# Output weights of seven kv heads read in 8 KB rows, results brought to that layout

## The chip, the cores and the metric

The kernel runs on one core of a Trainium2 chip. The metric is device time in microseconds (us) of one execution. Lower is better.

## The reference, cut to what matters

The program sums three terms for one decode step of a batch of 8: the input, grouped-query attention over a cache of 8192 positions, and a token mixer. Everything is float32.

```python
# B=8, D=512, Hq=32, Hkv=8, Sk=8192, Dh=128, F=1792; S=1 token
xn = layernorm(x)
q = (xn @ wq)                       # 32 heads of 128; 4 query heads share a kv head
scores = q . k * Dh**-0.5           # k_cache: (8, 8, 8192, 128), 268 MB
o = softmax(scores) @ v             # v_cache: the same size
attn = concat(o) @ wo               # wo: (4096, 512), 8.4 MB
h = layernorm(xn)
u = gelu(h * w1 + b1)               # for each of 512 channels, 1792 wide
y = sum(u * w2) + b2
out = x + attn + y
```

The two caches and the two weight matrices make 554 MB, each byte of which is read once.

## The kernel before

**Items and steps.** The work is cut into 64 items, one for each pair of kv head h and batch row b (item i = 8h + b). An item has one 4 MB tile of k and one of v. Partition p of such a tile holds 64 consecutive positions, that is 32 KB that lie in one piece in memory. An item is worked in four chunks of 16 positions a partition, and one chunk is one step of the main loop at the end of the kernel (256 steps and a few to run out). A step s calls `t_half` twice (TensorE transposes the k chunk s + 1, ScalarE and VectorE copy one half each out of PSUM), then `qk` (scores of chunk s), then `pv` (values of the chunk nine steps back, LAG = 9). Everything else is hung on a step and a place in it by `at(step, place, function)`: the softmax of an item (`sm_max`, `sm_bias`, `sm_exp`, `sm_place`, `sm_sum`), `o_place` two steps after the item's last `pv`, the projections `q_project`, `q_place` and `o_project` once for each kv head, and the mixer for batch row b = h (`mx_begin`, 14 times `mx_step`, `mx_end`). Each engine runs its instructions in this written order.

**Transfers.** All large loads are issued by SyncE, in one queue. The tiles `raw` of k and v come from a pool of five buffers (RING = 5), so that `load_next` (line 65) has up to five tiles under way or in use, and issues the next when `t_half` has done with a k tile or `pv` with a v tile. The queue also carries the query weights (`load_wq`, line 80) and the output weights (`load_wo`, line 86) of each kv head, 1 MB each, into one shared buffer `wqo`. A query weight row is a 2 KB piece. The output weights of one kv head are 512 rows of 512 numbers, and `load_wo` puts row r\*128 + p on partition p at place r: four separate pieces of 2 KB on each partition, one for each of the four query heads.

**From the values to the output.** `pv` leaves an item's result in PSUM in blocks (partition: position group, step and head; columns: four blocks of 128), ScalarE scales it by the softmax sum into `ob`, and `o_place` (line 294) sums the blocks that belong together. For each of the four blocks TensorE takes the 128x128 block as weights and four columns of the constant `ohu` as the moving operand, so that a 128x4 result has the 128 components of a head on the partitions and the four query heads in the columns. VectorE copies it to column `BS * b` of `OT[h]`. After the eight items of a kv head, `o_project` (line 305) multiplies `OT[h][:, r, :]` with `wos[h][:, r, :]` over r = 0 to 3 and adds the sum to `yacc`.

**Shared places.** PSUM has one buffer `misc` for all the small products, SBUF one buffer `sq` (the query rows of `q_project` and the scratch of `sm_bias`) and one buffer `g` (of `mx_step`). `mx_begin` spreads a normalized row over all partitions by one matmul with 8 partitions of `ident` as weights and the 512 columns of `hn` moving.

Of the kernel before, what the change touches and what calls it, by code (L numbers as in the profile page):

```python
# [8 lines left out]
F32 = mybir.dt.float32  # L9
AF = mybir.ActivationFunctionType  # L10
ALU = mybir.AluOpType
AX = mybir.AxisListType
PSUM = bass.MemoryType.PSUM

B, D, HQ, HKV, SK, DH, F = 8, 512, 32, 8, 8192, 128, 1792
REP = HQ // HKV
P = 128
# [3 lines left out]
CG = 4  # L21
GT = CH_T // CG
GW = P // CG
BS = GW // B
NC = D // P
# [13 lines left out]
def attn_mixer_kernel(ctx: ExitStack, tc: tile.TileContext, x, kc, vc, wq, wo, w1, b1, w2, b2, out):  # L39
    nc = tc.nc  # L40
    const = ctx.enter_context(tc.tile_pool(name="const", bufs=1))
    ring = ctx.enter_context(tc.tile_pool(name="ring", bufs=RING))
    ktp = ctx.enter_context(tc.tile_pool(name="ktp", bufs=2))
    work = ctx.enter_context(tc.tile_pool(name="work", bufs=2))
    one = ctx.enter_context(tc.tile_pool(name="one", bufs=1))
# [6 lines left out]
    def misc():  # L52
        return ps_m.tile([P, 512], F32, name="misc")
# [31 lines left out]

    def load_wo(h):
        t = one.tile([P, REP, D], F32, name="wqo")
        nc.sync.dma_start(t, wo[h * REP * DH:(h + 1) * REP * DH, :].rearrange("(r p) n -> p r n", p=P))
        wos[h] = t

    load_next()
# [14 lines left out]
    quarter = [slice(j * D // CG, (j + 1) * D // CG) for j in range(CG)]  # L106


    ident = const.tile([P, P], F32, name="ident")
# [8 lines left out]
    nc.vector.tensor_scalar(hmask, ohw, 1.0, 3.0e38, op0=ALU.subtract, op1=ALU.mult)  # L118
    ohu = const.tile([P, GT * REP], F32, name="ohu")
    nc.vector.tensor_reduce(ohu, ident.rearrange("p (j x) -> p x j", x=GW)[:, :GT * REP, :], AX.X, ALU.add)  # L120
    oh2 = work.tile([P, REP], F32, name="oh2")
    nc.vector.tensor_reduce(oh2, ident.rearrange("p (g x) -> p x g", x=2 * REP)[:, :REP, :], AX.X, ALU.add)
    lmask = const.tile([P, 1], F32, name="lmask")
# [2 lines left out]
    nc.vector.tensor_scalar(ohl, ohw, lmask, None, op0=ALU.mult)  # L126
    epst = const.tile([B, 1], F32, name="epst")
    nc.vector.memset(epst, EPS)
    bsel = const.tile([P, B, GW], F32, name="bsel")
    nc.vector.memset(bsel, 0.0)  # L130
    for b in range(B):
        nc.vector.memset(bsel[:, b, BS * b:BS * b + 1], 1.0)
    spread = const.tile([B, GW], F32, name="spread")
    nc.vector.memset(spread, 0.0)
    nc.vector.tensor_copy(spread.rearrange("b (c s) -> b c s", s=BS)[:, :, 0], ident[:B, :B])
# [6 lines left out]
    for k in range(2):  # L142
        t = const.tile([P, PW + GW - GT * REP], F32, name=f"pt{k}")
# [3 lines left out]
    for k in range(2):  # L147
        t = const.tile([P, REP, GW], F32, name=f"ot{k}")
# [4 lines left out]
    def layer_norm(dst, src):  # L153
        st = work.tile([B, 6], F32, name="st")
        nc.vector.bn_stats(st, src)
        mv = work.tile([B, 2], F32, name="mv")
        nc.vector.bn_aggr(mv, st)
        sd = work.tile([B, 1], F32, name="sd")
        nc.scalar.activation(sd, mv[:, 1:2], AF.Sqrt, bias=epst)
        rs = work.tile([B, 1], F32, name="rs")  # L160
        nc.vector.reciprocal(rs, sd)
        nc.vector.tensor_scalar(dst, src, mv[:, 0:1], rs, op0=ALU.subtract, op1=ALU.mult)

    xn = t2k.tile([B, D], F32, name="t2k")
    layer_norm(xn, x_sb)
    hn = const.tile([B, D], F32, name="hn")
    layer_norm(hn, xn)
    yx = t2k.tile([B, D], F32, name="t2k")
    nc.vector.tensor_scalar(yx, x_sb, b2t, None, op0=ALU.add)
# [122 lines left out]
    OT = {}  # L292

    def o_place(i):
        h, b = divmod(i, B)
        if b == 0:
            OT[h] = OTS[h % 2]
        m = misc()
        ob = OB.pop(i)
        for u in range(GT):  # L300
            nc.tensor.matmul(m[:, :REP], ob[:, u * DH:(u + 1) * DH], ohu[:, u * REP:(u + 1) * REP],  # L301
                             start=(u == 0), stop=(u == GT - 1))
        nc.vector.tensor_copy(OT[h][:, :, BS * b], m[:, :REP])
# [10 lines left out]
    mx = {}  # L314

    def mx_begin(b):
        m = misc()
        nc.tensor.matmul(m, ident[:B, b:b + 1].to_broadcast([B, P]), hn, start=True, stop=True)  # L318
        hb = one.tile([P, D], F32, name="hb")
        nc.scalar.copy(hb, m)  # L320
        acc = one.tile([P, D], F32, name="macc")
        nc.gpsimd.memset(acc, 0.0)
        mx[b] = (hb, acc)
# [8 lines left out]
    def mx_end(b):  # L332
        m = misc()
        for j in range(CG):
            nc.tensor.matmul(m[j * GW:(j + 1) * GW, :D // CG], bsel[:, b, :], mx[b][1][:, quarter[j]],
                             start=True, stop=True)
        nc.vector.tensor_add(yacc, m[:, :D // CG], yacc)

# [6 lines left out]
    for i in range(N_IT):  # L345
        s = (i + 1) * NCH
        at(s - 1, 2, sm_max, i)
        at(s, 3, sm_bias, i)
        at(s + 1, 1, sm_exp, i)
        at(s + 1, 3, sm_place, i)  # L350
        at(s + 2, 3, sm_sum, i)
        at(s + LAG + (2 if i < N_IT - 2 else 0), 3, o_place, i)
    HS = B * NCH
    for h in range(HKV):
        s = h * HS
        if h + 1 < HKV:
            at(s + LAG + 4, 3, load_wq, h + 1)
            at(s + LAG + 9, 2, q_project, h + 1)
            at(s + LAG + 10, 2, q_place, h + 1)
        at(s + LAG + 12, 3, load_wo, h)  # L360
        at(s + HS + LAG + 3, 2, o_project, h)
        at(s + 3, 2, mx_begin, h)
        for k in range(NF):
            at(s + 4 + k + k // 2, 1 + 2 * (k % 2), mx_step, h, k)
        at(s + 28, 2, mx_end, h)
# [5 lines left out]
    m = misc()  # L371
    for c in range(NC):
        nc.tensor.transpose(m[:, c * B:(c + 1) * B], xn[:, c * P:(c + 1) * P], ident[:B, :B])
    nc.vector.tensor_copy(xnT[:, :, :B], m[:, :NC * B].rearrange("p (c b) -> p c b", b=B))
    for j in range(CG):
        nc.tensor.matmul(m[j * GW:(j + 1) * GW, GT * GW:GT * GW + D // CG], spread, yx[:, quarter[j]], start=True, stop=True)
    nc.vector.tensor_copy(yacc, m[:, GT * GW:GT * GW + D // CG])
# [41 lines left out]
```

## Time and profile before

| | |
|---|---|
| median of three runs | 1308.89 us (1308.6 to 1309.88) |
| profiled execution | 1308.48 us |
| its span, first to last instruction | 1306.7 us |
| mean granted TensorE clock | 0.957 |
| DMA | 555.13 MB in 28164 packets, mean 425 GB/s |

The profile is one execution. "Busy" of an engine is the time in which it has an instruction at work. PE is TensorE, PEld its weight loads, DVE is VectorE, ACT is ScalarE, POOL is GpSimd and SP is SyncE. A DMA is cut into packets, one for each piece that is contiguous on both sides, and the packets of a DMA are shared out over 16 DMA engines. The share of a DMA queue is the time that its packets took, divided by 16 times the length of the stretch.

### The profile page before, as it was taken

Reading aid. Unit: us, or ns where it says so; the run is one execution under the profiler, and the core shown is the slowest. Engines: PE = TensorE matmul, PEld = TensorE weight load, DVE = VectorE, ACT = ScalarE, POOL = GpSimd, SP = SyncE. Lnnn points to the kernel's source line nnn. Section 1 sums busy time; section 2 is a strip of 40 time slices with the busy share of each in tenths; the row PEclk is TensorE's granted clock in tenths of the full one; section 3 lists DMA queues with packets and bytes.
Section 4 is the critical chain, followed back from the end, with each engine's and each line's share of the span. In section 5 each row is a group of like instructions: output and inputs, shape, how many; then the busy total and the mean of one; then the engine's idle time right before and its main releaser. Section 6 shows DMA issues by size and latency. Waiting matters only on the chain.

```text
span 1306.7 us, 22347 instructions
## 1 busy us (share of the span) xinstructions
PE 1162.4 (89%) x9852; PEld 715.8 (55%) x9852; DVE 407.4 (31%) x646; ACT 587.8 (45%) x740; POOL 227.0 (17%) x242
## 2 busy tenths in 40 slices
PE   6979899798998989979898898998989979899988
PEld 4545555455554655546555555554645546555554
DVE  4423233232332333323333233322323323233321
ACT  2654244552545525445254452554525535255532
POOL 1322002220122201222012220122201221012310
PEclk8999999998999999999999898999989989899999
DMA  9999999999999999999999999999999999999995
GB/s 402 432 431 431 428 430 432 429 429 433 432 431 428 429 431 432 432 433 427 433 432 430 430 429 433 433 431 429 429 431 430 433 429 432 432 432 432 432 427 223
DMA packets 28164, 555.13 MB, mean 425 GB/s; under 512 B 2556, under 2 KB 2588, under 8 KB 11172
## 3 DMA queue, kind: packets, MB, share of 16 engines
q1 hardware_dynamic: 27924, 553.67, 98.8%
q8 instruction: 77, 1.26, 0.4%
q14 instruction: 19, 0.16, 0.0%
q0 software_dynamic: 128, 0.02, 0.0%
q10 hardware_dynamic: 16, 0.02, 0.0%
HBM read 553.69 MB, written 0.02 MB: 424 GB/s over the span
## 4 chain that ended last, share of the span: by engine, by line
DMA 56%; PE 39%; ACT 3%; DVE 1%; issue 1%; POOL 0%; SPq 0%; ACTq 0%; DVEq 0%; POOLq 0%
DMA raw<-in_A_k_cache_dram 37%; DMA wqo<-in_A_wq_dram 17%; PE pt L202 16%; PE acc L220 8%; PE acc L276 8%; PE misc L301 3%; DMA raw<-in_A_v_cache_dram 3%; PE misc L177 1%; ACT L242 1%; PE misc L249 1%; ACT kt L203 1%; ACT t2k L242 1%; PE misc L318 1%; PE misc L257 1%; PE misc L309 1%
## 5 line engine op out<-in xcount | busy, mean ns | idle before, releaser
L202 PE MATMUL pt<-ident,raw 128*128 128x128 f32 x4096 | 515.9, 281 | 67.6 <-DMA raw<-in_A_k_cache_dram 67.1
L202 PEld LDWEIGHTS pt<-ident,raw 128*128 128x128 f32 x4096 | 478.0, 147 | 74.5 <-issue 56.0
L203 DVE COPY kt<-pt 128x1024 f32<-128x1024 f32 x256 | 313.5, 1225 | 618.3 <-PE pt L202 505.4
L203 ACT COPY kt<-pt 128x1024 f32<-128x1024 f32 x256 | 258.8, 1011 | 455.7 <-PE pt L202 322.9
L220 PE MATMUL acc<-kt,z 128*32 128x512 f32 x2048 | 279.0, 617 | 0.0
L276 PE MATMUL acc<-raw,pt 128*32 128x512 f32 x2040 | 273.0, 608 | 2.5 <-DMA raw<-in_A_v_cache_dram 2.5
L329 POOL TENSOR_SCALAR g<-g,w2t 128x512 f32<-128x512 f32 x112 | 77.5, 692 | 876.6 <-ACT g L328 876.6
L276 PEld LDWEIGHTS acc<-raw,pt 128*32 128x32 f32 x2040 | 65.3, 113 | 143.6 <-issue 118.1
L330 POOL TENSOR_TENSOR macc<-macc,g 128x512 f32<-128x512 f32 x112 | 142.3, 1271 | 9.3
L328 ACT ACTIVATE g<-hb,b1t,w1t 128x512 f32<-128x512 f32 x112 | 91.1, 813 | 11.5 <-POOL macc L330 10.9
L289 ACT ACTIVATE t2k<-acc,rl 128x512 f32<-128x512 f32 (+1 forms) x65 | 44.0, 679 | 108.5 <-PE acc L276 104.6
L301 PEld LDWEIGHTS misc<-ohu,t2k 128*128 128x128 f32 x512 | 61.9, 191 | 55.0 <-DVE kt L203 31.0
L249 PEld LDWEIGHTS misc<-ident,t2k 128*128 128x128 f32 x256 | 26.8, 140 | 82.5 <-ACT t2k L242 76.7
L301 PE MATMUL misc<-ohu,t2k 128*128 128x4 f32 x512 | 67.3, 255 | 0.7 <-ACT t2k L289 0.6
L220 PEld LDWEIGHTS acc<-kt,z 128*32 128x32 f32 x2048 | 40.7, 109 | 44.5 <-issue 44.4
L249 PE MATMUL misc<-ident,t2k 128*128 128x128 f32 x256 | 42.0, 286 | 25.5 <-ACT t2k L242 25.5
L242 ACT ACT_TABLE_LOAD x48 | 61.6, 1283 | 0.8
L328 ACT ACT_TABLE_LOAD x48 | 61.6, 1283 | 0.8
L257 PEld LDWEIGHTS misc<-lr,ohl 128*128 128x128 f32 x128 | 20.1, 197 | 59.1 <-issue 50.7
L177 PE MATMUL misc<-wqo,xnT 128*32 128x128 f32 x256 | 15.5, 420 | 38.8 <-DMA wqo<-in_A_wq_dram 38.3
L250 ACT COPY pt<-misc 128x256 f32<-128x256 f32 x64 | 23.7, 370 | 58.1 <-PE misc L249 58.1
L233 PEld LDWEIGHTS misc<-ident,mr 128*128 128x128 f32 x128 | 19.0, 187 | 53.7 <-DVE kt L203 38.6
(67 smaller groups left out, 285.6 us busy)
## 6 DMA issues: line engine op xcount, KB each, us to landing
raw<-in_A_k_cache_dram SPq DMA_DIRECT2D x63, 4096.0 KB, 30.0
raw<-in_A_v_cache_dram SPq DMA_DIRECT2D x63, 4096.0 KB, 33.2
wqo<-in_A_wq_dram SPq DMA_DIRECT2D x8, 1024.0 KB, 30.6
wqo<-in_A_wo_dram SPq DMA_DIRECT2D x8, 1024.0 KB, 28.3
raw<-in_A_k_cache_dram SPq DMA_DIRECT2D x4, 1024.0 KB, 10.2
raw<-in_A_v_cache_dram SPq DMA_DIRECT2D x1, 2048.0 KB, 29.1
raw<-in_A_v_cache_dram SPq DMA_DIRECT2D x1, 1024.0 KB, 31.2
raw<-in_A_v_cache_dram SPq DMA_DIRECT2D x1, 512.0 KB, 31.9
```

The source lines that it names most:

```text
L202: nc.tensor.transpose(pt[:, t * P:(t + 1) * P], KR[n // NCH][:, n % NCH * CH_T + k * w + t, :], ident)
L203: (nc.vector.tensor_copy if k else nc.scalar.copy)(KT[n][:, k * w * P:(k + 1) * w * P], pt)
L220: nc.tensor.matmul(S[i][j * GW:(j + 1) * GW, :], w, kt[:, j * 512:(j + 1) * 512], start=(c == 0), stop=(c == NCH - 1))
L242: nc.scalar.activation(p, S.pop(i), AF.Exp, bias=st[i], scale=SCALE, accum_out=lr)
L249: nc.tensor.transpose(m[:, u * P:(u + 1) * P], p[:, u * P:(u + 1) * P], ident)
L257: nc.tensor.matmul(m[:, :1], ohl, st.pop(i)[1], start=True, stop=True)
L276: nc.tensor.matmul(O[i][j * GW:(j + 1) * GW, :], w, v[:, j * 512:(j + 1) * 512], start=(c == 0), stop=(c == NCH - 1))
L289: nc.scalar.activation(ob[:, x], o[:, x], AF.Copy, scale=rl)
L301: nc.tensor.matmul(m[:, :REP], ob[:, u * DH:(u + 1) * DH], ohu[:, u * REP:(u + 1) * REP], start=(u == 0), stop=(u == GT - 1))
L328: nc.scalar.activation(g, hb, AF.Gelu_apprx_tanh, bias=b1t[:, j:j + 1], scale=w1t[:, j:j + 1])
L329: nc.gpsimd.tensor_scalar(g, g, w2t[:, j:j + 1], 1.0, op0=ALU.mult, op1=ALU.mult)
L330: nc.gpsimd.tensor_add(acc, acc, g)
```

## The change

`load_wo` reads the weights of the first seven kv heads so that partition p holds the rows 4p to 4p + 3, which lie together in memory: one piece of 8 KB a partition. The last kv head keeps the old layout. `OT[h]` must follow: partition p now stands for head p // 32 and components 4 (p mod 32) to 4 (p mod 32) + 3. For these heads `o_place` takes a new constant matrix `pick` (128x128 for each block) as the weights and the block itself, 128 columns, as the moving operand. This gives a 128x128 result in which row p holds all 128 components of head p // 32. A mask `keep` lets four of them stand, and a sum over strided columns brings them to 128x4.

Room in SBUF for `pick` and `keep` comes from two edits. The constant `bsel` becomes one strip that is read at a shifting offset in place of eight copies, and `hn` becomes a passing tile in the buffer of `g`. For that the rows of `hn` are transposed at the start to `hnT` (four small transposes and a copy), and `mx_begin` spreads a row with four matmuls with a 128x128 weight each and 128 columns of `ident` moving.

```diff
@@ load_wo
         t = one.tile([P, REP, D], F32, name="wqo")
-        nc.sync.dma_start(t, wo[h * REP * DH:(h + 1) * REP * DH, :].rearrange("(r p) n -> p r n", p=P))
+        how = "(r p) n -> p r n" if h == HKV - 1 else "(p r) n -> p r n"
+        nc.sync.dma_start(t, wo[h * REP * DH:(h + 1) * REP * DH, :].rearrange(how, p=P))
         wos[h] = t
@@ constants
+    pick = const.tile([P, GT, P], F32, name="pick")
+    nc.vector.tensor_copy(pick.rearrange("p u (h g) -> p (u h) g", h=REP),
+                          ohu.unsqueeze(2).to_broadcast([P, GT * REP, GW]))
+    own = work.tile([P, GW], F32, name="own")
+    nc.vector.tensor_reduce(own, ident.rearrange("p (j x) -> p x j", x=GW), AX.X, ALU.add)
+    keep = const.tile([P, P], F32, name="keep")
+    nc.vector.tensor_copy(keep.rearrange("p (g c) -> p g c", c=REP), own.unsqueeze(2).to_broadcast([P, GW, REP]))
@@
-    bsel = const.tile([P, B, GW], F32, name="bsel")
+    BO = BS * (B - 1)
+    bsel = const.tile([P, BO + GW], F32, name="bsel")
     nc.vector.memset(bsel, 0.0)
-    for b in range(B):
-        nc.vector.memset(bsel[:, b, BS * b:BS * b + 1], 1.0)
+    nc.vector.memset(bsel[:, BO:BO + 1], 1.0)
@@
-    hn = const.tile([B, D], F32, name="hn")
+    hn = one.tile([B, D], F32, name="g")
@@ o_place
         m = misc()
         ob = OB.pop(i)
+        if h < HKV - 1:
+            for u in range(GT):
+                nc.tensor.matmul(m[:, :DH], pick[:, u, :], ob[:, u * DH:(u + 1) * DH],
+                                 start=(u == 0), stop=(u == GT - 1))
+            t = one.tile([P, P], F32, name="sq")
+            nc.vector.tensor_tensor(t, m[:, :DH], keep, op=ALU.mult)
+            nc.vector.tensor_reduce(OT[h][:, :, BS * b], t.rearrange("p (g c) -> p c g", c=REP), AX.X, ALU.add)
+            return
         for u in range(GT):
@@ mx_begin
-        nc.tensor.matmul(m, ident[:B, b:b + 1].to_broadcast([B, P]), hn, start=True, stop=True)
+        for c in range(NC):
+            nc.tensor.matmul(m[:, c * P:(c + 1) * P], hnT[:, c, b:b + 1].to_broadcast([P, P]), ident, start=True, stop=True)
@@ mx_end
-            nc.tensor.matmul(m[j * GW:(j + 1) * GW, :D // CG], bsel[:, b, :], mx[b][1][:, quarter[j]],
+            nc.tensor.matmul(m[j * GW:(j + 1) * GW, :D // CG], bsel[:, BO - BS * b:BO - BS * b + GW], mx[b][1][:, quarter[j]],
@@ before the main loop
+    hnT = const.tile([P, NC, B], F32, name="hnT")
+    for c in range(NC):
+        nc.tensor.transpose(m[:, P + c * B:P + (c + 1) * B], hn[:, c * P:(c + 1) * P], ident[:B, :B])
+    nc.vector.tensor_copy(hnT, m[:, P:P + NC * B].rearrange("p (c b) -> p c b", b=B))
```

## Rows read from the trace of the kernel before

**Rows 1.** The page: engines' busy time; GB/s in 40 slices; packets; queues.
```profile
PE 1162.4 (89%) x9852; PEld 715.8 (55%) x9852; DVE 407.4 (31%) x646; ACT 587.8 (45%) x740; POOL 227.0 (17%) x242
...
GB/s 402 432 431 431 428 430 432 429 429 433 432 431 428 429 431 432 432 433 427 433 432 430 430 429 433 433 431 429 429 431 430 433 429 432 432 432 432 432 427 223
DMA packets 28164, 555.13 MB, mean 425 GB/s; under 512 B 2556, under 2 KB 2588, under 8 KB 11172
...
q1 hardware_dynamic: 27924, 553.67, 98.8%
q8 instruction: 77, 1.26, 0.4%
```
**Rows 2.** TensorE in the list of waits: who waited for whom, total us, times, longest.
```profile
PE pt L202 <- DMA raw<-in_A_k_cache_dram: 67.1, 31, 5.6
...
PE misc L177 <- DMA wqo<-in_A_wq_dram: 38.3, 7, 6.2
```
**Rows 3.** DMAs issued from 110 to 111 us: KB each, us to landing.
```profile
raw<-in_A_k_cache_dram SPq DMA_DIRECT2D x1, 4096.0 KB, 25.9
wqo<-in_A_wo_dram SPq DMA_DIRECT2D x1, 1024.0 KB, 28.1
```
**Rows 4.** SyncE's issues: start, us, what.
```profile
26.26 0.33 SPq L72 DMA_DIRECT2D raw<-in_A_v_cache_dram  x1
...
110.11 0.33 SPq L72 DMA_DIRECT2D raw<-in_A_k_cache_dram  x1
110.49 0.73 SPq L88 DMA_DIRECT2D wqo<-in_A_wo_dram  x1
```
**Rows 5.** The chain that ended last, its end: start, us, what.
```profile
1242.59 36.84 DMA raw<-in_A_v_cache_dram
...
1279.57 1.06 PE acc L276 x8
...
1303.24 0.29 DVE yacc L311
```
**Rows 6.** The DMA view, 135.6 to 136.2 us (0.6 us), within an output weight load.
```profile
DMA packets 120, 0.25 MB, mean 410 GB/s; under 512 B 0, under 2 KB 0, under 8 KB 120
...
q1 hardware_dynamic: 120, 0.25, 105.0%
```
**Rows 7.** The DMA view, 9.0 to 10 us, within the first k tile (quarters).
```profile
DMA packets 50, 0.41 MB, mean 410 GB/s; under 512 B 0, under 2 KB 0, under 8 KB 0
...
q1 hardware_dynamic: 50, 0.41, 96.6%
```
**Rows 8.** Groups by line and shape: count, busy us, mean ns, idle before.
```profile
L301 PE MATMUL misc<-ohu,t2k 128*128 128x4 f32 x512 | 67.3, 255 | 0.7 <-ACT t2k L289 0.6
...
L233 PE MATMUL misc<-ident,mr 128*128 128x128 f32 x128 | 31.2, 326 | 0.0
...
L303 DVE COPY ot<-misc 128x4 f32<-128x4 f32 x64 | 10.6, 166 | 80.0 <-PE misc L301 80.0
L318 PE MATMUL misc<-hn,ident 8*128 8x512 f32 x16 | 9.0, 639 | 0.0
...
L311 DVE TENSOR_TENSOR yacc<-misc,yacc 128x128 f32<-128x128 f32 x8 | 2.3, 292 | 5.5 <-PE misc L309 5.5
...
L113 DVE TENSOR_REDUCE oh<-ident 128x4 f32<-128x128 f32 x1 | 0.4, 381 | 3.2 <-POOL ident masks.py:199 3.2
```
**Rows 9.** Timeline, last item of a kv head: start, us, engine, what, [idle before].
```profile
222.35 0.17 DVE L303 COPY ot<-misc 128x4 f32<-128x4 f32 x1 [0.96 <-PE misc L301]
...
224.21 1.22 DVE L203 COPY kt<-pt 128x1024 f32<-128x1024 f32 x1 [1.69 <-PE pt L202]
224.50 0.13 PEld L309 LDWEIGHTS misc<-wqo,ot 128*32 128x32 f32 x4 [0.30 <-issue]
```
**Rows 10.** A stretch near the end: engines' busy us (count), clock, DMA share, GB/s.
```profile
1280.00:1290.00 10.00, 10.00 (x88) 4.88 (x80) 2.55 (x6) 2.29 (x4) 0.00 (x0) 1.00 0.76 320
```

## The prediction, made before the changed kernel was run

> **What bounds the kernel now.** I read the page first. Its row of GB/s shows one rate from the second slice to the last but one: 427 to 433 GB/s in every slice, with no dip where a kv head ends. The queue of SyncE (q1) alone accounts for 98.8% of the time of all 16 DMA engines, while TensorE's busy time is 89% and VectorE's 31% [rows 1]. So the reader should see a stream that never pauses.
>
> The waits say on which side the slack lies. TensorE waits 67.1 us in total for k tiles and 38.3 us for query weights [rows 2], 105 us in 64 items, or 1.65 us an item. TensorE catches up with the stream and then waits for it. A little more work on TensorE, VectorE or ScalarE shortens such a wait first.
>
> The queue is deep enough to keep it so. The k tile issued at 110.11 us landed 25.9 us later, and the 1 MB of output weights issued at 110.49 landed after 28.1 us [rows 3, 4]. A 4 MB tile takes 4.19 / 430 = 9.8 us at the stream's rate, so it had some 16 us of other transfers ahead of it. An issue may come that much later before the stream runs dry.
>
> Then the end. The last part of the chain is the transfer of a v tile from its issue at 1242.59 to 1279.4 us, then TensorE from 1279.57, and the last sum on VectorE at 1303.24 [rows 5]. All seven changed weight loads lie ahead of that v tile in the same queue. Whatever they save, the landing moves earlier by as much, and the work behind it, which belongs to the last kv head and is not changed, moves with it. The time is therefore the start, plus the sum of the packets on the slowest DMA engine, plus a fixed tail.
>
> **The change part by part.**
>
> *The transfer.* A kv head's output weights are 512 pieces of 2 KB now and 128 pieces of 8 KB afterwards. Each of the 16 engines carries 32 of the one or 8 of the other. The trace has both sizes. In a stretch of 0.6 us within such a load there are 120 packets, all of 2 KB, with a share of 105.0% [rows 6]: 1.050 x 16 x 0.6 / 120 = 84.0 ns a packet. The first k tile comes in quarters whose pieces are 8 KB; in 1 us there are 50 of these with 96.6% [rows 7]: 0.966 x 16 / 50 = 309 ns. Four small ones make 336 ns, so each 8 KB gains 27 ns. An engine carries 8 such pieces in a load and there are 7 loads: 56 x 27 = 1.51 us.
>
> A second reading bounds it. The weights landed at 110.49 + 28.1 = 138.6 us and the k tile ahead of them at 110.11 + 25.9 = 136.0 [rows 3, 4], so the 1 MB took 2.6 us with an error of 0.1. At 430 GB/s it would be 2.44 us. That is 0.06 to 0.26 us a load, 0.4 to 1.8 us for seven. I take 1.51 and keep 0.4 to 1.8 for the range.
>
> The Trainium skill, "DMA: Bandwidth & Descriptors", section Specifications, puts the least size for line rate at 512 B. By that both sizes run at line rate and the transfer gains nothing. The rows disagree: 84.0 ns for 2 KB is 24.4 GB/s on an engine and 309 ns for 8 KB is 26.5, some 8% apart [rows 6, 7].
>
> *`o_place`, 56 of 64 items.* TensorE issues the same four products. The moving operand grows from 4 to 128 columns. A matmul record of the present line averages 255 ns, one of the softmax bias, which moves 128 columns through 128x128 weights, 326 [rows 8]. There are 8 records an item. The cost is between nothing (the weight loads set the pace either way) and 8 x 71 ns = 0.57 us, over 56 items 0 to 32 us. Since records overlap, I take 0.1 us an item, 6 us. VectorE does a product out of PSUM (292 ns, the row of that shape at L311) and a strided sum (381 ns, L113) in place of a copy of 166 ns [rows 8]: 0.51 us more an item, 28 us.
>
> Is that on the path? At the end of a kv head the copy into `OT` starts at 222.35 us; the next VectorE instruction starts at 224.21 and the weight loads of `o_project`, which need `OT`, at 224.50 [rows 9]. The new pair ends at 222.35 + 0.67 = 223.0, with about 1.2 us to spare before the one and 1.5 before the other. Behind it on VectorE stands only the copy of a `t_half`, which waits for TensorE. `misc` is held 0.13 us longer and `sq` has no other user in that place. Cost on the path: 0. If the cover were gone, 56 x (0.51 + 0.1) = 34 us (61 us with the high price on TensorE), still under the 105 us for which TensorE now waits on the stream [rows 2].
>
> *`mx_begin`, 8 times.* Two records of 512 columns (639 ns each, 16 in all [rows 8]) become eight of 128 columns. At 326 ns each this is 2.6 us against 1.3, before overlap: 0 to 1.3 us for a kv head, 10 us in all at most, under the same slack. Cost: 0.
>
> *Start.* Two copies, a reduction, four small transposes and a copy come in and seven small fills go out. The dearest of these is no more than some 0.7 us and all together no more than 2 us, an estimate from the reduction at L113 (0.38 us for 128x128 in [rows 8]) and the copies of a `t_half` (1.22 us for twice the columns of `pick`, [rows 9]). They delay the release of the first buffer, seen in the issue at 26.26 us [rows 4]. At that time the queue held five tiles and 1 MB, 22 MB or 51 us at 430 GB/s, so about 25 us of stream were left. Cost: 0. If the cover were gone: 2 us.
>
> *Code.* TensorE gets 8 x 12 + 8 = 104 more instructions (products and weight loads). q8 moves 1.26 MB in 77 packets while TensorE has 2 x 9852 instructions [rows 1]: 64 B for each, if the queue is TensorE's alone, which I infer from this number. 104 of them are 6.7 KB, 0.4 of a packet. A packet costs one DMA engine 0.004 x 16 x 1306.7 / 77 = 1.1 us. The engines don't end together: from 1280 to 1290 us the share has fallen to 0.76 while data still come [rows 10], so a packet counts only on an engine that ends late. Between 0 and 1.1 us; I take half of 0.4 x 1.1, 0.2 us.
>
> *Sum.* -1.5 + 0.2 = -1.3 us. The profiled execution took 1308.48 us, which becomes 1307.2. The median of the runs is 0.4 above that execution, so on their scale 1308.89 becomes **1307.6**. A run of this kernel can tell about 0.2%, 2.6 us, from no change, and the forecast lies inside.
>
> **The rivals.**
>
> *Nothing is gained* (1308.9). An engine that sets the end may meet another code packet (1.1 us against 1.5), or the new rows may run no better than the old. For it speaks the lower bound of the landing reading (0.4 us); against it that both packet sizes are in the trace with different rates. The Trainium skill's rule on 512 B gives the same time. Chance 0.15.
>
> *More is gained* (1306 or less). If a weight load now holds up the stream beyond its own packets, on the engines that lag, the gain exceeds the sum. The landings cap what this one load could give at 0.26 us, so 1.8 us for seven, 1307.1; for a gain over 2.6 us each load would have to save 0.37 us. Later loads I take to be like this one. Chance 0.10.
>
> *Slower* (over 1311.5). TensorE becomes the bound: the longer `o_place`, with its wait for VectorE, comes to stand in the path. It decides once it adds more than the 1.65 us an item that TensorE waits now. My high price is 0.57 + 0.51 = 1.08 us an item. Should the slack be unusable, because it lies where tiles land late and not where `o_place` runs, then 56 x 0.61 = 34 us would be added: 1308.9 + 34 - 1.5, about 1341. For it speaks that TensorE is busy 89%; against it the even 430 GB/s and 16 us of queue. Chance 0.06.
>
> *The forecast*: the gain of the packets and hardly anything else. Chance 0.69.
>
> **How the numbers follow.** The forecast with its bounds is 1308.9 - 1.8 = 1307.1 to 1308.9 - 0.4 + 1.1 = 1309.6, and the three runs before spread from -0.3 to +1.0 around their median. With the rivals beside it on both sides I give 1305.0 to 1310.2. Faster by over 0.2% needs the larger gain: 0.11, with a little from runs that fall low. Slower by over 0.2%: 0.07. The rest, 0.82, within.
>
> **What would show it.** The page after should count 7 x 384 = 2688 packets fewer on q1 and the same bytes. A stretch within a weight load should show 8 KB packets of 309 ns. GB/s stays at 427 to 433. VectorE's busy time grows by some 28 us, TensorE's by 0 to 40, and TensorE's waits for k and query weights shrink by about what its own work grows. The tail, from the landing that is now at 1279.4 us, keeps its 24 us to the last sum. The prediction is wrong if the GB/s row dips, if SyncE's loads land within less than 15 us of issue (a stream run dry), or if the span falls by more than 2.6 us.

## The result: slower by 0.4%, and the profile after

The changed kernel takes 1314.06 us (median of six runs, 1313.56 to 1314.41) against 1308.86 for the kernel before (six runs): a ratio of 1.004, interval 1.003 to 1.005. The forecast was 1307.6, with a range up to 1310.2. The time moved the other way, and by more than the range allowed.

The page after, with the lines that answer to [rows 1] (the profiled execution took 1314.01 us):

```profile
span 1312.1 us, 22540 instructions
...
PE 1164.4 (89%) x9904; PEld 723.3 (55%) x9904; DVE 437.1 (33%) x699; ACT 587.8 (45%) x740; POOL 227.1 (17%) x242
...
GB/s 400 430 429 430 430 428 429 429 426 433 431 431 425 430 429 430 430 426 430 431 432 431 427 427 433 429 429 426 431 431 432 431 429 428 431 429 430 430 424 215
DMA packets 25478, 555.15 MB, mean 423 GB/s; under 512 B 2556, under 2 KB 2588, under 8 KB 7588
...
q1 hardware_dynamic: 25236, 553.67, 98.6%
q8 instruction: 78, 1.28, 0.4%
```

The rows did become larger: q1 has 2688 packets fewer for the same bytes. The stream still never pauses, but its rate is lower almost everywhere: 423 GB/s in the mean instead of 425, and 430 in slices that had 432. A loss of 0.4% spread evenly over the whole span is not a wait in one place. The waits of TensorE say the same, since they are what they were in [rows 2]:

```profile
PE pt L211 <- DMA raw<-in_A_k_cache_dram: 70.2, 34, 5.7
...
PE misc L186 <- DMA wqo<-in_A_wq_dram: 37.3, 7, 5.9
```

TensorE still waits for these two in the stream, 107.5 us in all against 105.4. The end shows where the time arrived. The v tile whose landing began the tail in [rows 5] is issued at 1249.81 us now, in the list of SyncE's issues, and the DMA view of 1249 to 1260 us has its time to landing; the chain ends with the same sum on VectorE.

```profile
1249.81 22.16 SPq L72 DMA_DIRECT2D raw<-in_A_v_cache_dram  x7
```
```profile
raw<-in_A_v_cache_dram SPq DMA_DIRECT2D x1, 4096.0 KB, 34.3
```
```profile
1308.66 0.29 DVE yacc L328
```

The landing is at 1284.1 us, 4.7 later than before. But it no longer begins the tail. The last transfer in the chain is now the k tile ahead of it; the product with the v tile (L285) starts at 1285.02 and waits for nothing. A line of the chain, two of TensorE's timeline and the 4 us behind the first of them in the view by windows (the clock is the third number from the end), all of the changed kernel:

```profile
1242.91 28.72 DMA raw<-in_A_k_cache_dram
```
```profile
1271.76 3.57 PE L211 MATMUL pt<-ident,raw 128*128 128x128 f32 x16 [1.93 <-DMA raw<-in_A_k_cache_dram]
...
1285.02 1.04 PE L285 MATMUL acc<-raw,pt 128*32 128x512 f32 x8
```
```profile
1272.00:1276.00 4.00, 4.00 (x24) 3.29 (x27) 0.58 (x1) 1.01 (x1) 0.00 (x0) 0.61 1.07 452
```

In the kernel before, the same k tile is issued at 1235.69 us; here are its time to landing (the DMA view of 1235 to 1236 us) and the timeline:

```profile
raw<-in_A_k_cache_dram SPq DMA_DIRECT2D x1, 4096.0 KB, 31.4
```
```profile
1267.26 1.94 PE L202 MATMUL pt<-ident,raw 128*128 128x128 f32 x16 [0.28 <-DMA raw<-in_A_k_cache_dram]
...
1279.57 1.06 PE L276 MATMUL acc<-raw,pt 128*32 128x512 f32 x8 [0.50 <-DMA raw<-in_A_v_cache_dram]
```

The k tile lands at 1242.91 + 28.72 = 1271.6 us instead of 1235.69 + 31.4 = 1267.1, which is 4.5 us later. From there to the last sum it is 37.0 us instead of 36.1. At the start of this part TensorE had waited 1.93 us for the tile. Its granted clock over the next 4 us was 0.61 on average, mostly the lower of its two levels (1.2 and 2.4 GHz), where it was 1.00 before, and 16 transposes took 3.57 us instead of 1.94. Most of the 5.4 us by which the last sum is later lies in the stream ahead of the landings, and 0.9 us behind them.

The next question is what a packet takes. In 140 to 250 us no weights are moved, only k and v tiles. The DMA view of that stretch, first before the change, then after:

```profile
DMA packets 1632, 47.52 MB, mean 432 GB/s; under 512 B 176, under 2 KB 176, under 8 KB 176
...
q1 hardware_dynamic: 1622, 47.38, 100.0%
```
```profile
DMA packets 1624, 47.26 MB, mean 430 GB/s; under 512 B 176, under 2 KB 176, under 8 KB 176
...
q1 hardware_dynamic: 1614, 47.12, 99.8%
```

Before, 1622 - 176 = 1446 packets of 32 KB share 16 x 110 = 1760 us of engine time (the 176 smallest, at 9 ns each in the trace, take 1.6 of it): 1216 ns each. After, 1438 packets share 0.998 x 1760 = 1756.5 us, less the same 1.6: 1220 ns. The error of each is 0.6 ns, from the last digit of the share. **Packets of k and v, which the change doesn't touch, take 4 ns longer.** An engine carries 1008 of them, which makes 4 us.

The weights' packets are longer too. Two stretches within a load of query weights (2 KB packets), 93.0 to 95.0 us before and 93.4 to 95.4 after, in the same view:

```profile
DMA packets 342, 0.69 MB, mean 343 GB/s; under 512 B 7, under 2 KB 7, under 8 KB 342
...
q1 hardware_dynamic: 342, 0.69, 88.3%
```
```profile
DMA packets 328, 0.66 MB, mean 329 GB/s; under 512 B 7, under 2 KB 7, under 8 KB 328
...
q1 hardware_dynamic: 328, 0.66, 88.5%
```

335 packets in 0.883 x 32 us are 84.2 ns each, 321 in 0.885 x 32 are 88.0. Again about 4 ns, for a packet of a sixteenth of the size.

One thing that every packet has, and that the change could reach, is the place it is written to. The new constants `pick`, `keep` and `hnT` and the smaller `bsel` and `hn` change what lies in SBUF ahead of the ring of `raw` buffers and of `wqo`. In the compiled programs, the first `raw` buffer starts at byte 29440 of each partition before (115 x 256) and at 29312 after (114 x 256 + 128). The buffers are 32 KB long, so all five share that remainder. `wqo` starts 64 past a multiple of 256 before and 192 past one after.

### The profile page after: what moved, and what is told of

It is laid out like the page before. It is cut to its first block, busy times and chain, and to the rows that moved or that the text cites. A ratio compares the mean times of both kernels' runs of the same rounds, so it can differ in the third digit from the quotient of the medians.

```text
span 1312.1 us, 22540 instructions
## 1 busy us (share of the span) xinstructions
PE 1164.4 (89%) x9904; PEld 723.3 (55%) x9904; DVE 437.1 (33%) x699; ACT 587.8 (45%) x740; POOL 227.1 (17%) x242
## 4 chain that ended last, share of the span: by engine, by line
DMA 56%; PE 39%; ACT 3%; DVE 1%; issue 1%; POOL 0%; SPq 0%; ACTq 0%; DVEq 0%; POOLq 0%
DMA raw<-in_A_k_cache_dram 39%; DMA wqo<-in_A_wq_dram 16%; PE pt L211 16%; PE acc L229 8%; PE acc L285 8%; PE misc L311 3%; PE misc L186 1%; ACT L251 1%; PE misc L258 1%; ACT kt L212 1%; ACT t2k L251 1%; PE misc L336 1%; PE misc L266 1%; PE misc L326 1%; PE misc L318 0%
## 5 line engine op out<-in xcount | busy, mean ns | idle before, releaser
L285 PE MATMUL acc<-raw,pt 128*32 128x512 f32 x2040 | 272.8, 607 | 3.4 <-DMA raw<-in_A_v_cache_dram 3.4
L285 PEld LDWEIGHTS acc<-raw,pt 128*32 128x32 f32 x2040 | 65.5, 113 | 140.0 <-issue 115.3
L311 PEld LDWEIGHTS misc<-t2k,pick 128*128 128x128 f32 x448 | 54.2, 191 | 47.9 <-DVE kt L212 27.7
L311 PE MATMUL misc<-t2k,pick 128*128 128x128 f32 x448 | 64.7, 287 | 0.0
L268 DVE RECIPROCAL rl<-misc 128x1 f32<-128x1 f32 x64 | 10.8, 168 | 114.7 <-PE misc L266 114.6
```

What stands on the lines that cost most here:

```text
L285: nc.tensor.matmul(O[i][j * GW:(j + 1) * GW, :], w, v[:, j * 512:(j + 1) * 512], start=(c == 0), stop=(c == NCH - 1))
L311: nc.tensor.matmul(m[:, :DH], pick[:, u, :], ob[:, u * DH:(u + 1) * DH], start=(u == 0), stop=(u == GT - 1))
```

## The experiments

**Theory A**: a packet takes longer when its buffer starts off a multiple of 256 bytes. **Theory B**: the longer `o_place` and `mx_begin`, or their code, cost the time. **Theory C**: the 8 KB rows slow the stream. Each run below was timed beside the kernel before, whose medians were 1308.72 to 1308.82 us.

### Moving the ring

In the changed kernel, `hnT` goes to a pool that lies behind the ring:

```diff
-    hnT = const.tile([P, NC, B], F32, name="hnT")
+    hnT = one.tile([P, NC, B], F32, name="hnT")
```

> The changed kernel with one word different: hnT (128 bytes a partition) is taken from the pool that lies behind the ring of raw tiles, so that the five raw buffers start at byte 29184 of each partition, a multiple of 256, as they did before the change (29440), and not at 29312, which is 128 past one. All instructions are the same. Theory A (where the raw buffers start sets how long their packets take): the packets of k and v go back to a mean of about 1216 ns from 1220 and the time falls to about 1307.4 us, that of before less the 1.5 us of the larger rows, faster than before by about 0.1%. Theory B (the longer o_place and mx_begin on TensorE and VectorE, or one more code packet, cost the time): 1314 us, as the changed kernel. Theory C (the 8 KB rows themselves slow the stream): 1314 us.

Measured: **1307.53 us**, ratio 0.9992 (0.9983 to 1.0001). The whole loss is gone with one word, and what remains is the forecast, 1307.6. B and C fall here: the longer code and the 8 KB rows are still in this kernel. The expectation overlooks that the edit also moves `wqo`, from 192 to 64 past a multiple. So this run alone doesn't say which of the two buffers matters; later ones do. It also speaks for 256 and not for 512 as the multiple: the ring starts at 114 x 256 here and at 115 x 256 in the kernel with the large rows alone (below), and the two run alike (1307.53 and 1307.44 us).

The reverse, in the kernel before, is an unused constant ahead of the ring:

```diff
     xnT = const.tile([P, NC, GW], F32, name="xnT")
+    const.tile([P, 32], F32, name="pad")      # 16 and 8 columns in the other two runs
```

> The kernel before with an unused constant of 128 bytes a partition ahead of the ring, so that the raw buffers start 128 bytes past a multiple of 256 (29568); nothing else is changed. Theory A: slower than before by what the changed kernel lost, 5.2 us, and the 1.5 us that its larger rows gave: about 1315.5 us. Theories B and C: 1308.9 us, no change.

> The kernel before with an unused constant of 64 bytes ahead of the ring: the raw buffers start 64 past a multiple of 256. Theory A with any start off a multiple of 256 costing the same: about 1315.5 us. Theory A with only some remainders costing (128 alone, by a fault of place that is not the 256): 1308.9 us. Theories B and C: 1308.9 us.

> The kernel before with an unused constant of 32 bytes ahead of the ring: the raw buffers start 32 past a multiple of 256 and also off a multiple of 64. Theory A with any start off a multiple of 256 costing the same: about 1315.5 us; if a start off a multiple of 64 costs more still: above 1317 us. Theories B and C: 1308.9 us.

Measured: **1315.15** (ratio 1.0047, 1.0034 to 1.0060), **1315.32** (1.005, 1.0038 to 1.0063) and **1316.33 us** (1.0058, 1.0045 to 1.0070). An unused constant of 32 to 128 bytes makes the old kernel 6.4 to 7.6 us slower. 128 past is no special place: 64 costs the same, and 32 some 1 us more. These edits move `wqo` along with the ring, to 192, 128 and 96 past a multiple.

### The parts of the change, with the ring on a multiple

The large rows alone, in the kernel before:

```diff
-        ... .rearrange("(r p) n -> p r n", p=P))
+        ... .rearrange("(r p) n -> p r n" if h == HKV - 1 else "(p r) n -> p r n", p=P))
```

> The kernel before with one part of the change alone: the output weights of seven kv heads are read in 8 KB rows; o_place, mx_begin and all buffers stay as they were (raw at byte 29440, a multiple of 256). The output sums of these heads pair values with the wrong rows of the weights. Theory A with the packets' own lengths: 1308.8 less 56 x 27 ns = 1307.3 us. Theory C (the rows slow the stream): 1309 us or more. If the rows give nothing: 1308.8 us.

Everything else alone, in the kernel with `hnT` moved:

```diff
-        how = "(r p) n -> p r n" if h == HKV - 1 else "(p r) n -> p r n"
+        how = "(r p) n -> p r n"
```

> The rest of the change alone, with the ring at a multiple of 256 (29184): the new o_place, mx_begin, bsel and hn, but all output weights in 2 KB rows as before. The output sums of seven heads pair values with the wrong rows of the weights. Theory A: 1308.8 us or up to 0.5 us more by the one code packet more, that is, the 28 us of new work on VectorE and what TensorE has more are hidden. Theory B (this work is on the path): 1309.5 us and more.

Measured: **1307.44 us** for the rows (ratio 0.999, 0.998 to 0.9999) and **1308.82** for the rest (1.0002, 0.9993 to 1.0011). The rows give 1.3 us by the medians, and all the added work of TensorE, VectorE and code together nothing that can be seen.

### Which buffer

`own` is put into the buffer `sq` to make room, and an unused `pad` of the pool in front of `wqo` sets where that starts; the ring is moved by the place of `hnT` or a small constant. The core of the edits:

```diff
     ident = const.tile([P, P], F32, name="ident")
+    work.tile([P, 24], F32, name="pad")       # 24, 16 or 8 columns
...
-    own = work.tile([P, GW], F32, name="own")
+    own = one.tile([P, P], F32, name="sq")[:, :GW]
```

> The changed kernel with the ring at a multiple of 256 (29184) and also the weight buffer wqo (at 210176; in the kernel before and in the run with the ring moved back it stands 64 past a multiple). If each packet pays for the start of its own buffer, the 2 KB and 8 KB packets of the weights are shorter by some 2 ns each: 312 of them an engine, 0.6 us, about 1306.9 us. If what counts is the ring alone: 1307.5 us. Theories B and C: 1314 us.

> The changed kernel with the ring left at 128 past a multiple of 256 (29312), and the weight buffer wqo moved to a multiple of 256 (210176). If each packet pays for the start of its own buffer, the packets of the weights are back at 84 and 309 ns (86 to 88 and 313 in the changed kernel) and the time is 1314.1 less some 0.9 us, about 1313.2. If the weights' packets are slowed by the k and v packets that run beside them, nothing changes: 1314.1 us. If the start of wqo is what cost the changed kernel its time: 1307.5 us.

> The changed kernel with the ring at a multiple of 256 (29184) and the weight buffer wqo 192 past a multiple (210112), where the changed kernel has it. It separates the two buffers, which the run with the ring moved back moved together (ring 128 to 0, wqo 192 to 64 past a multiple). If the two add up: with both at a multiple 1306.8, and wqo at 192 costs the 3.3 us that its move gained with the ring off: 1310.1 us. If wqo costs only beside a ring that is off: 1307.5 us or less. If all of the cost were the ring's, 1306.8.

> As the run before it, with wqo 128 past a multiple of 256 (210048). If every start off a multiple of 256 costs alike: the same time as with 192. If 64 past is the only cheap one of them (wqo at 64 with the ring on gave 1307.5): 1310 us here as with 192. If cost grows with the distance: between 1307.5 and 1310.1 us.

> The changed kernel with the ring 64 past a multiple of 256 (29248) and wqo at a multiple (210176). If any start of the ring off a multiple of 256 costs the same: 1310.8 us, as with the ring 128 past one and wqo on a multiple. If 64 past is nearly free, as it is for wqo: 1307.5 us or less.

Measured, in us, all with the same instructions on the engines (the first column gives where the ring starts past a multiple of 256):

| ring | `wqo` on a multiple | `wqo` off it |
|---|---|---|
| on a multiple | **1306.84** (0.9988, 0.9978 to 0.9997) | 1307.53 (64 past), 1307.40 (128), 1307.43 (192) |
| 64 past | 1311.48 (1.0022, 1.0013 to 1.0031) | not run |
| 128 past | 1310.81 (1.0017, 1.0008 to 1.0026) | 1314.06 (192 past, the changed kernel) |

Off in `wqo` alone costs 0.6 us, the same for three starts. That is inside the intervals; but of the eleven runs with both on a multiple six are below 1306.9 us, and of the 33 with `wqo` alone off none is below 1307.1. Off in the ring alone costs 4.0 to 4.6. Both off cost 7.2, which is 2.6 more than 4.0 and 0.6. So of what was expected of the run with the ring on and `wqo` at 192, the branch by which the two add up (1310.1 us) failed, and the branch by which `wqo` costs beside a ring that is off (1307.5 or less) held, up to the 0.6. At 128, `wqo` costs what it costs at 192. The gain of moving `wqo` beside a ring that is off had been put at 0.9 us; it is 3.3.

Does a packet pay for the start of its own buffer? The traces say: not simply. First the weights' packets, in the same view. The lines are, in this order, the 2 KB packets with both on a multiple (93.0 to 94.8 us), with `wqo` alone off at 192 (93.0 to 95.0) and with the ring alone off at 128 (93.3 to 95.1):

```profile
q1 hardware_dynamic: 304, 0.61, 86.8%
```
```profile
q1 hardware_dynamic: 346, 0.69, 89.4%
```
```profile
q1 hardware_dynamic: 299, 0.60, 85.1%
```

Without the 7, 7 and 8 smallest packets that is 84.0, 84.2 and 84.0 ns, against 88.0 in the changed kernel, where both are off. Then the 8 KB rows, with both on a multiple (134.4 to 135.9 us), with `wqo` alone off at 192 (134.4 to 136.2) and in the changed kernel (135 to 136.7):

```profile
q1 hardware_dynamic: 73, 0.52, 82.7%
```
```profile
q1 hardware_dynamic: 85, 0.62, 81.8%
```
```profile
q1 hardware_dynamic: 78, 0.57, 80.0%
```

Nine packets of each are the smallest ones (0.08 us in all). The rest take 19.77 / 64 = 309 ns, 23.48 / 76 = 309 and 21.68 / 69 = 314. So in these loads a `wqo` that is off lengthens its packets by 4 to 5 ns when the ring is off too, and by 0.2 ns or less when the ring is on.

The packets of k and v depend on more than their own buffer as well. With the ring off and `wqo` on, and then with both on a multiple, the DMA view of 140 to 250 us has

```profile
DMA packets 1627, 47.36 MB, mean 431 GB/s; under 512 B 176, under 2 KB 176, under 8 KB 176
...
q1 hardware_dynamic: 1617, 47.22, 100.0%
```
```profile
DMA packets 1629, 47.44 MB, mean 431 GB/s; under 512 B 176, under 2 KB 176, under 8 KB 176
...
q1 hardware_dynamic: 1620, 47.32, 99.9%
```

1758.4 / 1441 = 1220 ns, as in the changed kernel, and 1756.6 / 1444 = 1216 ns. In 98 to 133 us, between a load of query weights and one of output weights, it is otherwise. The lines are the changed kernel, the ring alone off, and both on a multiple:

```profile
q1 hardware_dynamic: 506, 15.01, 99.8%
```
```profile
q1 hardware_dynamic: 507, 15.04, 99.8%
```
```profile
q1 hardware_dynamic: 509, 15.11, 100.1%
```

Each has 48 of the smallest packets (0.4 us). The rest of 16 x 35 = 560 us gives 1219, 1217 and 1215 ns, each with an error of 0.6. With `wqo` on a multiple, a ring that is off costs its packets under 2 ns here and 4 there. With both off, the packets are longer in each of these stretches. This is where the two buffers don't add up.

One rival stands. In every compiled program the buffers `kt` (the transposed k) start at the ring's remainder and `g` at that of `wqo`. No DMA of the caches or weights writes these, but no run moves them apart from the two landing buffers, so that it is the landing buffers is likely and not shown.

### For each packet, or for the bytes?

Each 4 MB tile is loaded by two DMAs, one for each half of a partition's row, with the ring on a multiple and off it (`wqo` is on one in both):

```diff
-... if last else (NT,):
+... if last else (NT // 2, NT // 2):
```

> The changed kernel with ring and wqo at multiples of 256 (1306.8 us), and each 4 MB tile of k and v loaded by two DMAs, one for each half of a partition's row, so that a packet has 16 KB and there are twice as many. It is the base for the run with the same halves and the ring off. A packet of 16 KB takes 611 ns and one of 32 KB 1213, so two cost 9 ns more before any overlap of a packet with the next: 1008 x (5 to 9) ns, 5 to 9 us more, about 1312 to 1316 us.

> As the run before it, with the ring 128 past a multiple of 256 and wqo on a multiple. With whole tiles this step cost 4.0 us. If the cost is one for each packet, whatever its length: 8 us over the run before it. If it goes with the bytes that are written: 4 us over it.

Measured: **1312.75 us** (1.0029, 1.0018 to 1.0039) and **1322.03** (1.0099, 1.0083 to 1.0114). The first is what was estimated for it, 5.9 us above whole tiles. The step from on to off is 9.3 us with packets of 16 KB and was 4.0 with 32 KB: twice the packets, more than twice the cost, with the same bytes. Even the lowest run with the ring off (1320.04) is 6.3 us above the highest with it on (1313.70), so a cost that goes with the bytes, 4 us, is out; one for each packet, 8 us, is the nearer. The packets of both in 140 to 250 us, on and then off:

```profile
DMA packets 3246, 47.25 MB, mean 430 GB/s; under 512 B 360, under 2 KB 360, under 8 KB 360
...
q1 hardware_dynamic: 3236, 47.12, 100.3%
```
```profile
DMA packets 3224, 46.97 MB, mean 427 GB/s; under 512 B 355, under 2 KB 355, under 8 KB 355
...
q1 hardware_dynamic: 3213, 46.83, 100.2%
```

1762.0 / 2876 = 612.7 ns and 1760.3 / 2858 = 615.9: 3.2 ns for a packet of 16 KB, against 4 for one of 32 KB in the same stretch. At 2016 packets an engine that is 6.5 of the 9.3 us; the rest isn't explained.

## Why the prediction was wrong, step by step

- **What bounds the kernel**: right. TensorE waits for a stream that never pauses, and whatever changes a packet's time moves the end.
- **The transfer, -1.51 us**: right. The rows alone gave 1.3 us, and the 8 KB packets take 309 ns in the runs with the ring on a multiple.
- **`o_place`, `mx_begin`, start, at nothing**: right. The run with all of these and none of the rows is at 1308.82. VectorE's busy time rose by 29.7 us (28 forecast) and TensorE's by 2.0. A record of the new product averages 287 ns, between the bounds of 255 and 326 [rows 8]. At the end of a kv head the pair on VectorE ends at 224.04 us and the copy behind it starts at 225.13. The group of the product, then the timeline:

```profile
L311 PE MATMUL misc<-t2k,pick 128*128 128x128 f32 x448 | 64.7, 287 | 0.0
```
```profile
223.31 0.29 DVE L314 TENSOR_TENSOR sq<-misc,keep 128x128 f32<-128x128 f32 x1 [1.06 <-PE misc L311]
223.64 0.40 DVE L315 TENSOR_REDUCE ot<-sq 128x4 f32<-128x128 f32 x1
225.13 1.23 DVE L212 COPY kt<-pt 128x1024 f32<-128x1024 f32 x1 [1.09 <-PE pt L211]
```

- **Code, +0.2 us**: TensorE has 104 instructions more and q8 one packet more, as worked out. Its cost is too small to see.
- **The sum failed by a term that it did not have.** It counted what the change does to the packets of the seven loads, took those of the 128 k and v tiles as given, and asked of the edits to `bsel`, `hn`, `pick` and `keep` only what their instructions cost. What they did besides was to move the ring off a multiple of 256, beside a `wqo` that was off one before and after. An engine's 1008 large packets lose 4 ns each (4.0 us), its 288 of 2 KB 3.8 ns (1.1 us) and its 56 of 8 KB 5 ns (0.3 us), 5.4 us. The runs say 6.5 (1314.06 against 1307.53, the run with the ring back on and `wqo` still off). So about 1 us has no place in this count. Part of it is the scatter of the runs: the two executions that were traced, 1314.01 and 1308.16 us, are 5.9 apart.
- **The fixed tail**: not quite. The sum hung it on the landing of a v tile; in the changed kernel TensorE doesn't wait for that tile, and the part behind the k tile took 0.9 us more.
- **The rivals**: the slower one named the wrong mechanism (TensorE as the bound), and none of them let the packets of k and v change.

The Trainium skill, "DMA: Bandwidth & Descriptors", section "How a descriptor splits into AXI transactions", says that a transaction must start on a 256 B boundary, and its table gives a descriptor of 576 B that starts off one four transactions where an aligned one has three. The page speaks of what a transaction reads; here the pieces of the source stayed where they were, and the destination in SBUF was moved. If the rule holds for a destination, each packet here would take one transaction more in a buffer that is off, whatever its length. The halves agree (3.2 ns for 16 KB, 4 for 32 KB). The weights' packets don't: with `wqo` alone off they take 84.2 and 309 ns, against 84.0 and 309 on a multiple. The page's count of beats doesn't agree either: by it a start 192 past would cost three times one of 64, an estimate from its rule, and the runs of `wqo` show the same time for both.

Open are three things: why the ring and `wqo` off together cost more than the sum of each alone, why the kernel before with the ring 32 bytes past costs 1 us more than with 64, and what in the DMA engine or SBUF takes the 4 ns. No run here tells that. What is shown is that the starts of the buffers, and no instruction, cost the time.

The version that beats both kernels is the changed one with both buffers on a multiple of 256: 1306.84 us, 0.15% below the kernel before.

## What to carry to other kernels

A kernel that lives on its DMA stream can have the start of its landing buffers as a hidden parameter; here it is worth up to 7.2 us of 1307. After any edit to the constants in SBUF, look at the remainder of their addresses by 256, and try a pad or another order of the pools that makes it zero. A loss that is spread evenly over the span, with the same waits and the same bytes, is seen in the time of a packet: divide a queue's share by its packets in a stretch that moves only one size, and take more than one stretch. And an edit that costs no instruction can still cost something, through what it moves in memory.

## What was not expected of the hardware

- With the ring and `wqo` both off a multiple of 256 bytes, packets from HBM take 4 to 5 ns longer than with both on one, whatever their size: 84.0 to 88.0 ns (2 KB), 309 to 314 (8 KB), 1216 to 1220 (32 KB). With the ring alone off, packets of 16 KB go from 612.7 to 615.9.
- It isn't a price that each packet pays for its own start. Weights that land off a multiple beside a ring on one take 84.2 and 309 ns, and k and v tiles in a ring that is off, beside a `wqo` on one, take 1220 ns in one stretch and 1217 in another.
